# The eighth b's softmax steps placed inside the h tiles of the last stage, its F ahead of the state's first logits

## The chip, the core and the metric

The kernel runs on one core of a Trainium2 chip. The metric is the device time of one execution in microseconds; less is better. The profiled execution is read with times counted from its first instruction. Engines: PE is TensorE (matmuls), DVE is VectorE, ACT is ScalarE, POOL is GpSimd, and SP issues nearly all the transfers.

## The reference, cut to what matters

```python
# attention between x (8 b, 512 tokens, 8 heads) and a state of 32 slots per b
a  = softmax over slots (x @ state^T / 8);   xread = a @ state
a2 = softmax over tokens(state @ x^T / 8);   sread = a2 @ x
x  = concat([xread, sread])          # per b 512 tokens and 32 state rows, 8 * 544 rows of 512
# dense layer
h  = x @ w_in                        # 2048 hidden
g  = 1 if h >= 1 else 0 if h <= -1 else (h + 1)^2 / 4
x  = g @ w_out
# soft mixture: 8 experts x 4 slots = 32 slots
logits = x @ phi
d  = softmax over all rows (logits);     slot_input = d^T @ x
slot_out = relu(slot_input @ w1[e]) @ w2[e]
c  = softmax over the slots (logits);    out = c @ slot_out
```

Since x is only used through phi and through d^T, the kernel never forms g @ w_out for all rows: it forms the logits from g and w_out @ phi, and sums d^T g over the rows before w_out is applied.

## The kernel before, in words

The rows are worked on in nine stages. Stages b = 0 to 7 hold the 512 token rows of one b each; the last stage, b = 8, holds the 256 state rows of all b. Each stage has 16 **h tiles** m (128 hidden units times the stage's rows). `hstep` makes one: matmuls into one of three PSUM buffers (pool `psH`, three in turn, so h(m) takes the buffer of h(m-3)), then the activation. In the last stage an h tile is 12 matmuls of 256 columns, k = 0 to 11, since weights and x are split in a high and a low half (`wsplit` makes the halves `w` of tile m+1: a cast for the high half and a subtraction for the low half, on the engines that a table names; there are two sets, used in turn). The activation there has one of three forms; for tiles 0, 2, 3 and 4 it is a TENSOR_SCALAR on DVE (L564), a square on ACT and a SCALAR_TENSOR_TENSOR on DVE (L597); for tiles 1, 5, 6 and 7 a relu on ACT, a product on POOL (L569) and a SCALAR_TENSOR_TENSOR on DVE (L593). The DVE instruction at the end writes g and is what frees the PSUM buffer.

`estep(b, k)` (tile **E**) makes the logits of b from four g tiles; four of them sum up. `smblock(b)` then does the softmax over rows as a running one, as a generator whose steps the stage loop calls:

1. eS, a copy of the logits to SBUF on ACT;
2. **LR**: four small matmuls that turn them; DVE takes the maximum **bm** and the running maximum **nm**; ACT makes the exponentials (eS again), al = exp(old maximum - new) and the copy LT; DVE updates the running sum **sn**;
3. **dRp**: four transposes of eS on PE, and their copy **dR** on ACT;
4. `fall`, **F**: 64 matmuls of dR with the b's transposed g (tile gp), into two banks of the PSUM pool psV (FV) and two buffers of psX (FX); then eight DVE instructions fold them into **acc** (L742);
5. after the eighth b (b = 7), `merge`: D, **Mp**, nmM, al, R4a and Ra, then the matmuls **P** and **Sp** on acc and sn.

In the last stage the eighth b's steps 1 to 5 are called after h tiles 1 to 5, one each. The state's own logits E of that stage follow after tiles 5, 8, 11 and at the end; `tquarter` (tile **gtp**, eight transposes for each four g tiles, into psV) follows after tiles 5, 9, 13 and at the end.

What is written in that order is not yet each engine's order: in the last stage a list scheduler sorts the instructions of each engine by its own estimate of when they could start, so matmuls of the next h tile may stand ahead of a step. Once sorted, each engine works its list strictly in order.

The transfers all go through SP's queue, in order: F's end frees gp, into which four loads of 1 MB of expert weights go at once; P's end frees acc; the last reader of a weight tile `win`, and in the end the matmuls of the state's own sums (also named P, there reading natS) free the places of the next loads. After the last stage come the state's softmax (`smstate`), the experts on the weights as they land, and the combination, whose results are written out.

Of the kernel before, what the change touches and what calls it, by code (L numbers as in the profile page):

```python
# [13 lines left out]
PSUM = bass.MemoryType.PSUM  # L14


CFG = {'gg': 1, 'ns': 1, 'do': 0, 'no': 1, 'nl': 0, 'n0': (1, 12), 'nw': 512, 'nj': 'CABD', 'cw': (2, 2, 2, 4, 5, 6, 6, 7, 8, 8, 9, 11, 12, 13, 14, 15), 'pr': (0, 3, 4, 6), 'a0n': 4, 'w1p': (), 'r0': 3, 'sw': 1, 'whole': (6, 7), 'em': 8, 'lE': (0, 5, 8, 11), 'sV': (0, 4, 9, 12), 'sE': (7, 11, 15), 'sS': (1, 3, 5, 7), 'sN': 13, 'sM': (14, 14), 'gv7': 'EESEESSEEESSEEEE', 'cpos': (0, 0, 1, 1, 2, 2, 3, 7, 8, 9, 10, 10, 13, 14), 'at0': (4, 4, 7, 7, 9, 13, 14, 15, 15, 15), 'lP0': ((1, 1), (2, 1), (3, 1)), 'lP1': ((1, 0), (1, 1), (2, 0), (2, 1), (3, 0)), 'gv1': 'EEEEEEEEEESEEEES', 'f32': (0, 1, 2, 3), 'wsm': 14, 'xsP': 1, 'eng': ('PE',), 'wt8': (7, 8, 9, 10, 11, 12, 13, 14), 'wte': 'DA', 'wb': 12, 'gv6': (3, 5, 15), 'lP': ((0, 0), (0, 1), (1, 0), (2, 0), (3, 1)), 'attA': (3, 4, 7, 9, 9, 9, 11, 12), 'attB': (1, 11, 11, 12, 13), 'attN': (14, 15), 'dv': (3, 7, 8), 'fl': -0.484375, 'hp': 2000, 'att7': (3, 5, 6, 7, 8, 10), 'og': 1, 'n3': 1, 'n3m': 10, 'wS': ('AP', 'PP', 'AD', 'AP', 'DP', 'DP', 'PP', 'DD', 'AP', 'DP', 'AD', 'AP', 'DD', 'AD', 'DD', 'DP'), 'xsm': 12, 'k0': 0, 'rg': 6, 'spg': 0, 'att0': 6, 'att': 7, 'V0': (1, 3, 4), 'Vn': (0, 3, 9), 'Vx': 12, 'wn': 'H', 'wsev': 'adad', 'conv': (4, 8, 9, 11, 12, 13, 19, 21, 24, 26, 28, 32, 36, 40, 44, 48, 52, 56, 60), 'todo': [1, 1, 1, 2, 0, 0, 0, 3, 0, 0, 2, 2, 1, 1, 0, 0], 'E0': ((0, 8), (0, 14), (0, 14), (0, 15)), 'T0': ((0, 12), (0, 14), (0, 15), (1, 0)), 'sm0': 6, 'E': 1, 'sm': 1, 'tqB': (5, 9, 13), 'GP': 0, 'pe': (3,), 'psH': 3, 'gtpX': (0, 7), 'tq0': (13, 15), 'keep': (2, 3, 4, 5), 'x2': (1, 3), 'natm': 1, 'warm': 26, 'bounce7': (0, 3), 'split': 1, 'wt': 0, 'so': '111000000000ccc111111', 'smm': (0, 0, 1, 2, 8, 10, 12), 'tqv': (), 'tqvm': 0, 'first': 'x', 'apath': 2, 'f32c': 1, 'place': 1, 'attm': (3, 6, 7, 8, 9, 12), 'subPm': True, 'loDm': False, 'bounce': (0, 1, 2, 3), 'bq': ('s', 's'), 'xq': 's', 'nat': ((1, 11), (2, 2), (2, 3), (2, 11), (3, 2), (3, 4), (3, 9), (4, 2), (4, 3), (4, 9), (5, 2), (5, 3), (5, 9), (6, 2), (6, 4), (6, 9)), 'subP': (1,), 'mulD': (), 'loD': (), 'qlag': 0, 'gv0': 'ESSESEEESEEEEEEE', 'gv': 'EEEEEEESEEEESEEE', 'gvS': 'BEBBBEEESSSBEBBB'}


@with_exitstack  # L20
def kernel(
# [157 lines left out]
        stage_load(nxt(i))  # L179

    wps, wD = {}, {}

    def conv_wo(i):

        g, h = divmod(i - 8, 2)
        if h == 0:
            wD[g] = rot_g.tile([128, 4, 512], F32, tag="g", name="wD")
        words(i, wD[g][:, 2 * h:2 * h + 2, :].rearrange("p k f -> p (k f)"))
        stage_load(nxt(i))
        if h == 1:  # L190
# [333 lines left out]
    def hstep(b, m):  # L524
# [6 lines left out]
        elif b < B:  # L531
            vh, vl = Vt[b, c]
            ah, al = aT[b]
            f = slice(128 * mm_, 128 * mm_ + 128)
            seq = [(vh, ah), (vh, al), (vl, ah)]
            k = 0
            for G in range(2):
                for v, a in seq:
                    mm(out=h, lhsT=v[:, G, f], rhs=a[:, G, :], start=(k == 0), stop=(k == 5))  # L539
                    k += 1  # L540
        else:
            wh, wl = wS[m]
# [87 lines left out]
    def smblock(b):  # L630
# [89 lines left out]
    def fall(b, al, dR):  # L720
# [226 lines left out]
    for b in range(B + 1):  # L947
# [14 lines left out]
        for m in range(NM):  # L962
# [156 lines left out]
    def combine(dh, groups):  # L1119
# [4 lines left out]
        for n, bs in groups:  # L1124
# [80 lines left out]
```

## Time and profile before

| | us |
|---|---|
| median of 3 runs | 477.71 (477.70 to 478.51) |
| profiled execution | 476.62 |
| its span, first to last instruction | 474.8 |
| PE busy | 436.8 (92%) |
| DVE busy | 372.8 (79%) |
| ACT busy | 288.6 (61%) |
| POOL busy | 245.4 (52%) |

How to read it: "busy" is the time in which an engine has an instruction at work; PE overlaps its matmuls, so that its ends are modelled. The page cuts the span in 40 slices of 11.9 us and gives each engine's busy share in tenths. The chain of work that ended last is followed backwards from the last instruction, at each step to what released it. A row of the timeline gives start, length, engine, line and operation; what stands in brackets is the idle time before it and what ended it. Most rows name a line of a helper (L128 is every ACT instruction, L116 and L122 are matmuls issued side by side, L820 is every load of expert weights).

### The profile page before, as it was taken

The numbers are of one execution on the slowest core, as the hardware profiler recorded it, in microseconds if no ns is written. First come the engines' busy times: TensorE is split into PE (matmuls) and PEld (weight loads), VectorE is DVE, ScalarE is ACT, GpSimd is POOL, SyncE is SP. The second block draws the span as 40 slices with busy tenths as digits, with TensorE's granted clock in tenths as the row PEclk, the third lists the DMA queues.
The fourth block names the chain that finished last, engine by engine and source line by source line (L and its number), as shares of the span: only waits on it lengthen the run. The fifth ranks groups of instructions, "written<-read, shape, count | busy, mean of one in ns | idle before, by whom it ended". The sixth has DMA issues, their size and how long they took to land.

```text
span 474.8 us, 10761 instructions
## 1 busy us (share of the span) xinstructions
PE 436.8 (92%) x4352; PEld 249.5 (53%) x4352; DVE 372.8 (79%) x664; ACT 288.6 (61%) x526; POOL 245.4 (52%) x222
## 2 busy tenths in 40 slices
PE   4699999999999999999999999999999998899860
PEld 2433345455565565565556555655656786436430
DVE  2999999896999998999899999977877665350350
ACT  1868987647784875887587588545745364210350
POOL 4243347865873973796397379645247542030030
PEclk9889899999999999999999999999999999999995
DMA  8999822010403613260361326106045399999998
GB/s 300 420 420 418 362 90 90 11 80 13 167 1 135 232 79 135 90 222 10 130 247 62 134 90 233 79 19 249 1 179 186 126 373 353 342 421 418 388 357 273
DMA packets 21634, 94.21 MB, mean 198 GB/s; under 512 B 1873, under 2 KB 8401, under 8 KB 13265
## 3 DMA queue, kind: packets, MB, share of 16 engines
q1 hardware_dynamic: 21328, 93.00, 51.9%
q8 instruction: 34, 0.56, 0.5%
q0 software_dynamic: 256, 0.52, 0.4%
q14 instruction: 16, 0.12, 0.1%
HBM read 80.41 MB, written 13.11 MB: 197 GB/s over the span
## 4 chain that ended last, share of the span: by engine, by line
PE 51%; DVE 29%; DMA 7%; issue 4%; POOL 3%; ACT 2%; ACTq 0%; SPq 0%; POOLq 0%; DVEq 0%
PE h L539 19%; DMA w<-in_w_dram 6%; DVE gp L618 6%; DVE g L593 5%; PE h L547 5%; PE E L116 4%; PE FV L122 4%; PE V L116 3%; PE FX L122 2%; PE h L530 2%; POOL c L569 2%; DVE mx L295 2%; PE FV L116 1%; DVE win L173 1%; DVE z L336 1%
## 5 line engine op out<-in xcount | busy, mean ns | idle before, releaser
L539 PE MATMUL h<-a,v 128*128 128x512 f32 x672 | 175.2, 404 | 2.0 <-DVE g L593 1.7
L569 POOL TENSOR_TENSOR c<-c 128x512 f32<-128x512 f32 x107 | 116.8, 1095 | 99.7 <-ACT c L128 97.9
L539 PEld LDWEIGHTS h<-a,v 128*128 128x128 f32 x672 | 120.3, 188 | 77.2 <-issue 19.7
L128 ACT ACTIVATE c<-h,half 128x512 f32<-128x512 f32 x128 | 88.2, 690 | 71.7 <-PE h L539 55.8
L593 DVE SCALAR_TENSOR_TENSOR g<-h,c 128x512 f32<-128x512 f32 x112 | 74.7, 668 | 19.7 <-POOL c L569 16.9
L618 DVE STREAM_TRANSPOSE gp<-g 128x512 f32<-128x512 f32 x112 | 78.2, 700 | 1.2
L486 POOL TENSOR_TENSOR v<-Vs,v 128x512 fp32r<-128x512 f32 x30 | 41.7, 1389 | 9.3 <-ACT Vs L128 9.3
L128 ACT ACTIVATE v<-V 128x512 fp32r<-128x512 f32 (+1 forms) x64 | 38.1, 602 | 6.8 <-PE V L122 3.8
L116 PE MATMUL V<-win,st_t 64*32 64x512 f32 x64 | 33.4, 601 | 4.0 <-ACT att L128 3.5
L122 PE MATMUL V<-win,st_t 64*32 64x512 f32 x448 | 35.7, 601 | 0.0
L530 PE MATMUL h<-spare,v 128*128 128x512 f32 x64 | 34.0, 669 | 1.8 <-DVE gp L593 0.8
L122 PE MATMUL FX<-gp,dR 32*32 32x512 f32 x512 | 35.6, 598 | 0.0
L122 PE MATMUL FV<-gp,dR 32*32 32x512 f32 x496 | 35.4, 597 | 0.0
L122 PE MATMUL E<-g,wp 128*32 128x512 f32 x168 | 29.5, 602 | 0.0
L116 PE MATMUL E<-g,wp 128*32 128x512 f32 x56 | 29.1, 602 | 0.0
L338 POOL TENSOR_TENSOR att<-att,z 128x512 f32<-128x512 f32 x16 | 17.2, 1077 | 18.1 <-DVE z L337 18.1
L547 PE MATMUL h<-XSh,v 128*128 128x256 f32 x128 | 25.2, 289 | 0.0
L1141 DVE COPY o<-oV 128x512 f32<-128x512 f32 x6 | 4.1, 692 | 26.6 <-PE oH L122 26.5
L128 ACT ACTIVATE spare<-wb 128x512 uint8<-128x512 uint8 x32 | 23.9, 784 | 0.0
L530 PEld LDWEIGHTS h<-spare,v 128*128 128x128 f32 x64 | 12.2, 207 | 20.8 <-issue 12.9
L547 PEld LDWEIGHTS h<-XSh,v 128*128 128x128 f32 x128 | 20.3, 189 | 2.8 <-issue 1.0
L1149 POOL DMA_DIRECT2D out_dram<-o x8 | 4.1, 518 | 31.8 <-DVE o L1141 31.8
(245 smaller groups left out, 829.9 us busy)
## 6 DMA issues: line engine op xcount, KB each, us to landing
w<-in_w_dram SPq DMA_DIRECT2D x22, 1024.0 KB, 10.1
xn<-in_xn_dram SPq DMA_DIRECT2D x8, 1024.0 KB, 4.8
wb<-in_won_dram SPq DMA_DIRECT2D x8, 1024.0 KB, 5.0
xs<-in_xs_dram SPq DMA_DIRECT2D x7, 1024.0 KB, 5.1
gp<-in_w_dram SPq DMA_DIRECT2D x6, 1024.0 KB, 6.8
out_dram<-o SPq DMA_DIRECT2D x12, 512.0 KB, 6.5
gp<-in_wout_dram SPq DMA_DIRECT2D x5, 1024.0 KB, 12.2
wb<-in_win_dram SPq DMA_DIRECT2D x4, 1024.0 KB, 13.6
```

Of the source, the lines that this page charges most:

```text
L116: first = mm(**calls[0])
L122: e = mm(**c)
L128: return nc.scalar.activation(out=out, in_=in_, func=func, **kw)
L295: nc.vector.tensor_reduce(out=mx, in_=S[G], op=ALU.max, axis=AX.X)
L338: (nc.vector if b in CFG["mulD"] else nc.gpsimd).tensor_tensor(out=t3, in0=t3, in1=z1.unsqueeze(2).to_broadcast([128, 16, 32]), op=ALU.mult)
L486: nc.gpsimd.tensor_tensor(out=lo[:, G, :], in0=Vs, in1=hi[:, G, :], op=ALU.subtract)
L530: mm(out=h, lhsT=Vt[0, c][0][:, G, 128 * mm_:128 * mm_ + 128], rhs=araw[0][G], start=(G == 0), stop=(G == 1))
L539: mm(out=h, lhsT=v[:, G, f], rhs=a[:, G, :], start=(k == 0), stop=(k == 5))
L547: mm(out=h, lhsT=w[:, j, :], rhs=x[:, j, :], start=(k == 0), stop=(k == 11))
L569: nc.gpsimd.tensor_tensor(out=c, in0=c, in1=c, op=ALU.mult)
L593: gI[b, m] = nc.vector.scalar_tensor_tensor(out=g, in0=h, scalar=1.0, in1=c, op0=ALU.max, op1=ALU.min)
L618: nc.vector.transpose(out=gd_of(b, m), in_=gT[b, m])
```

## The change

Five table entries that are new (`ev`, `st`, `fa`, `fb`, `fd`) are off, and the code that they would switch on does nothing. What is left: in the last stage the eighth b's steps 2, 3 and 4 are no longer called after h tiles 2, 3 and 4 but from within an h tile's loop over its 12 matmuls, ahead of matmul k of tile m, at (2, 7), (4, 1) and (4, 10); that matmul is told to stand behind the step's last matmul on PE. Steps 1 and 5 stay after tiles 1 and 5.

```diff
-CFG = {'gg': 1, ...
+CFG = {'ev': 0, 'st': 0, 'fa': 0, 'fb': 0, 's8': ((2,7),(4,1),(4,10)), 's9': (1, 5), 'fd': (), 'gg': 1, ...
...
             for j in range(4):
                 for w, x in ((wh, xh), (wh, xl), (wl, xh)):
-                    mm(out=h, lhsT=w[:, j, :], rhs=x[:, j, :], start=(k == 0), stop=(k == 11))
+                    e = None
+                    if (m, k) in CFG["s8"]:
+                        step(run["sm"])
+                        e = run["pe"]
+                    i = mm(out=h, lhsT=w[:, j, :], rhs=x[:, j, :], start=(k == 0), stop=(k == 11))
+                    if e is not None:
+                        tc.add_manual_dep(i.ins, e.ins.name, ORDER, reason="in turn")
                     k += 1
...
-        group([dict(out=LR[32 * t:32 * t + 32, :], lhsT=R4, rhs=eS[:, 128 * t:128 * t + 128], start=True, stop=True) for t in range(T)])
+        run["pe"] = group([dict(out=LR[32 * t:32 * t + 32, :], lhsT=R4, rhs=eS[:, 128 * t:128 * t + 128], start=True, stop=True) for t in range(T)])
...
-            nc.tensor.transpose(dRp[:, r, :], eS[:, 128 * r:128 * r + 128], ident)
+            run["pe"] = nc.tensor.transpose(dRp[:, r, :], eS[:, 128 * r:128 * r + 128], ident)
...
-        group([dict(out=F[k][32 * t:32 * t + 32, :], lhsT=dR[32 * k:32 * k + 32, r, 32 * t:32 * t + 32],
+        run["pe"] = group([dict(out=F[k][32 * t:32 * t + 32, :], lhsT=dR[32 * k:32 * k + 32, r, 32 * t:32 * t + 32],
...
-                        sm = smblock(b - 1)
+                        sm = run["sm"] = smblock(b - 1)
...
-            if sm is not None and (m >= CFG["sm0"] if b == 1 else m >= CFG["sm"] if last or CFG["smm"] is None else m in CFG["smm"]):
+            if sm is not None and (m >= CFG["sm0"] if b == 1 else (m in CFG["s9"] if CFG["s8"] else m >= CFG["sm"]) if last else m in CFG["smm"]):
                 step(sm)
```

The instructions and their number stay the same on all engines; POOL's and SP's lists keep their order, and all lists are the same up to the second h tile of the last stage. In the names below h_3976, h_4003, h_4022, h_4056, h_4174, h_4243 and h_4261 are the last stage's h tiles 0, 1, 2, 3, 5, 6 and 7 in both kernels; tile 4 is h_4081 before and h_4074 now. The line numbers of the kernel now are 13 to 25 higher in these functions.

PE, last stage, where F begins. Before, tile 5 was complete, and the state's first logits (E_4190) stood ahead of F:

```order
L547 MATMUL h_4174<-XSl_3925,v0_568 128x256
L547 MATMUL h_4174<-XSh_3924,v0_568 128x256
L116 MATMUL E_4190<-s_gc_3971,wp_95 32x256
L122 MATMUL E_4190<-s_gc_3971,wp_95 32x256 x3
L116 MATMUL FV_4097<-gp_107,dR_4077 32x512
```

Now the same place of PE's list, from dRp on:

```order
L568 MATMUL h_4074<-XSh_3924,v0_568 128x256
L689 MATMUL dRp_4076<-cst_t_87,eS_101 128x128 x4
L568 MATMUL h_4074<-XSl_3925,v0_568 128x256
L568 MATMUL h_4074<-XSh_3924,v0_568 128x256 x2
L568 MATMUL h_4074<-XSl_3925,v0_568 128x256
L568 MATMUL h_4074<-XSh_3924,v0_568 128x256 x2
L568 MATMUL h_4074<-XSl_3925,v0_568 128x256
L568 MATMUL h_4074<-XSh_3924,v0_568 128x256 x2
L568 MATMUL h_4174<-XSh_3924,v0_568 128x256
L568 MATMUL h_4174<-XSl_3925,v0_568 128x256
L116 MATMUL FV_4092<-gp_107,dR_4081 32x512
```

F moved from behind tile 5 and E to behind ten matmuls of tile 4 and the first two of tile 5; the ten others of tile 5, E, and now also eight transposes gtp follow F.

DVE, last stage, the stretch from bm to the g of tile 3. Before:

```order
L520 CAST v0_568<-win1_104 128x512
L593 SCALAR_TENSOR_TENSOR s_gc_3971<-h_4003,s_gc_3971 128x256
L564 TENSOR_SCALAR s_gc_3971<-h_4022 128x256
L642 TENSOR_REDUCE bm_4043<-LR_4038 128x1
L651 SCALAR_TENSOR_TENSOR nm_4047<-bm_4043,nm_3691 128x1
L748 TENSOR_SCALAR D_4195<-cst_t_87,nm_4047 128x4
L520 CAST v0_568<-win1_104 128x512
L597 SCALAR_TENSOR_TENSOR s_gc_3971<-h_4022,s_gc_3971 128x256
L564 TENSOR_SCALAR s_gc_3971<-h_4056 128x256
L660 SCALAR_TENSOR_TENSOR sn_4051<-sn_3695,al_4046,bs_4045 128x1
```

The same stretch now (the first CAST is tile 4's high half, the second tile 5's; each is followed on POOL by the subtraction for the low half):

```order
L665 TENSOR_REDUCE bm_4035<-LR_4030 128x1
L616 SCALAR_TENSOR_TENSOR s_gc_3971<-h_4003,s_gc_3971 128x256
L674 SCALAR_TENSOR_TENSOR nm_4039<-bm_4035,nm_3691 128x1
L537 CAST v0_568<-win1_104 128x512
L587 TENSOR_SCALAR s_gc_3971<-h_4022 128x256
L771 TENSOR_SCALAR D_4195<-cst_t_87,nm_4039 128x4
L537 CAST v0_568<-win1_104 128x512
L587 TENSOR_SCALAR s_gc_3971<-h_4056 128x256
L683 SCALAR_TENSOR_TENSOR sn_4043<-sn_3695,al_4038,bs_4037 128x1
L620 SCALAR_TENSOR_TENSOR s_gc_3971<-h_4022,s_gc_3971 128x256
```

The casts stand behind bm and nm, and the instruction that ends tile 2 (reads h_4022, L597, now L620) moved from ahead of sn to behind it.

DVE, last stage, behind F's first fold into acc. Before, casts and g of tile 4 and 5 stood ahead of the fold:

```order
L597 SCALAR_TENSOR_TENSOR s_gc_3971<-h_4081,s_gc_3971 128x256
L520 CAST v0_568<-win1_104 128x512
L521 TENSOR_TENSOR v0_568<-win1_104,v0_568 128x512
L593 SCALAR_TENSOR_TENSOR s_gc_3971<-h_4174,s_gc_3971 128x256
L742 SCALAR_TENSOR_TENSOR acc_97<-acc_97,al_4046,FV_4097 128x8x32 x4
```

Now:

```order
L765 SCALAR_TENSOR_TENSOR acc_97<-acc_97,al_4038,FX_4094 128x8x32 x2
L587 TENSOR_SCALAR s_gc_3971<-h_4074 128x256
L537 CAST v0_568<-win1_104 128x512
L538 TENSOR_TENSOR v0_568<-win1_104,v0_568 128x512
L620 SCALAR_TENSOR_TENSOR s_gc_3971<-h_4074,s_gc_3971 128x256
```

Tile 4's activation and both halves of tile 7's weights moved behind the fold.

## Rows read from the trace of the kernel before

**Rows 1.** The page, 40 slices: busy tenths of PE and of the DMA engines.
```profile
PE   4699999999999999999999999999999998899860
DMA  8999822010403613260361326106045399999998
```

**Rows 2.** Stretches: busy us (count) of PE, PEld, DVE, ACT, POOL; clock; DMA share; GB/s.
```profile
406.50:407.50 1.00, 0.73 (x7) 0.36 (x4) 0.48 (x1) 0.33 (x1) 0.00 (x0) 1.00 0.37 156
409.50:441.00 31.50, 30.10 (x382) 14.26 (x374) 8.96 (x14) 5.08 (x11) 5.14 (x3) 1.00 1.01 409
```

**Rows 3.** SP's queue: its longest wait from 395 to 415 us, and two issues.
```profile
SPq L820 <- PE P L122: 6.0, 1, 6.0
...
379.47 0.33 SPq L820 DMA_DIRECT2D gp<-in_w_dram  x1
...
406.73 0.33 SPq L820 DMA_DIRECT2D w<-in_w_dram  x1
```

**Rows 4.** The chain that ended last, 367 to 390 us: start, us, what.
```profile
367.46 1.85 PE h L547 x14
369.31 0.23 PE LR L116
...
369.67 2.80 PE h L547 x22
372.47 0.44 PE dRp L666 x4
372.90 1.52 PE h L547 x12
374.43 0.33 PE E L116
...
375.00 0.54 PE FV L116
...
379.39 3.03 PE h L547 x24
382.42 0.65 PE gtp L613 x6
...
386.93 1.18 PE h L547 x10
...
389.38 0.71 PE h L547 x6
```

**Rows 5.** Timeline of POOL, the low halves of tiles 4 and 5 (L521), and an earlier product.
```profile
133.41 1.05 POOL L338 TENSOR_TENSOR att<-att,z 128x512 f32<-128x512 f32 x1
...
369.57 1.28 POOL L521 TENSOR_TENSOR v<-win,v 128x512 fp32r<-128x512 f32 x1 [0.62 <-DVE v L520]
371.63 1.29 POOL L521 TENSOR_TENSOR v<-win,v 128x512 fp32r<-128x512 f32 x1 [0.79 <-DVE v L520]
```

**Rows 6.** Timeline of DVE, instructions beside those of POOL, and the fold.
```profile
133.45 1.02 DVE L651 SCALAR_TENSOR_TENSOR nm<-bm,nm 128x1 f32<-128x1 f32 x1
...
369.00 0.43 DVE L520 CAST v<-win 128x512 fp32r<-128x512 f32 x1 [1.34 <-PE h L547]
...
369.67 0.42 DVE L564 TENSOR_SCALAR s_gc<-h 128x256 f32<-128x256 f32 x1
370.00 0.28 DVE L642 TENSOR_REDUCE bm<-LR 128x1 f32<-128x128 f32 x1
...
372.04 0.90 DVE L660 SCALAR_TENSOR_TENSOR sn<-sn,al,bs 128x1 f32<-128x1 f32 x1
...
379.40 1.66 DVE L742 SCALAR_TENSOR_TENSOR acc<-acc,al,FV 128x256 f32<-128x256 f32 x4 [2.89 <-PE FX L122]
...
382.54 0.72 DVE L520 CAST v<-win 128x512 fp32r<-128x512 f32 x1
...
385.56 0.68 DVE L521 TENSOR_TENSOR v<-win,v 128x512 fp32r<-128x512 f32 x1
```

**Rows 7.** Lines of DVE over the run: shortest, median and longest ns.
```profile
L660 DVE SCALAR_TENSOR_TENSOR sn<-sn,al,bs x7: 170/173/897, 136.3 to 372.0; 128x1 f32<-128x1 f32 x7
```

More of the change, by code (lines that the diff above doesn't have):

```diff
@@ new lines @@
+CFG = {'ev': 0, 'st': 0, 'fa': 0, 'fb': 0, 's8': ((2,7),(4,1),(4,10)), 's9': (1, 5), 'fd': (), 'gg': 1, 'ns': 1, 'do': 0, 'no': 1, 'nl': 0, 'n0': (1, 12), 'nw': 512, 'nj': 'CABD', 'cw': (2, 2, 2, 4, 5, 6, 6, 7, 8, 8, 9, 11, 12, 13, 14, 15), 'pr': (0, 3, 4, 6), 'a0n': 4, 'w1p': (), 'r0': 3, 'sw': 1, 'whole': (6, 7), 'em': 8, 'lE': (0, 5, 8, 11), 'sV': (0, 4, 9, 12), 'sE': (7, 11, 15), 'sS': (1, 3, 5, 7), 'sN': 13, 'sM': (14, 14), 'gv7': 'EESEESSEEESSEEEE', 'cpos': (0, 0, 1, 1, 2, 2, 3, 7, 8, 9, 10, 10, 13, 14), 'at0': (4, 4, 7, 7, 9, 13, 14, 15, 15, 15), 'lP0': ((1, 1), (2, 1), (3, 1)), 'lP1': ((1, 0), (1, 1), (2, 0), (2, 1), (3, 0)), 'gv1': 'EEEEEEEEEESEEEES', 'f32': (0, 1, 2, 3), 'wsm': 14, 'xsP': 1, 'eng': ('PE',), 'wt8': (7, 8, 9, 10, 11, 12, 13, 14), 'wte': 'DA', 'wb': 12, 'gv6': (3, 5, 15), 'lP': ((0, 0), (0, 1), (1, 0), (2, 0), (3, 1)), 'attA': (3, 4, 7, 9, 9, 9, 11, 12), 'attB': (1, 11, 11, 12, 13), 'attN': (14, 15), 'dv': (3, 7, 8), 'fl': -0.484375, 'hp': 2000, 'att7': (3, 5, 6, 7, 8, 10), 'og': 1, 'n3': 1, 'n3m': 10, 'wS': ('AP', 'PP', 'AD', 'AP', 'DP', 'DP', 'PP', 'DD', 'AP', 'DP', 'AD', 'AP', 'DD', 'AD', 'DD', 'DP'), 'xsm': 12, 'k0': 0, 'rg': 6, 'spg': 0, 'att0': 6, 'att': 7, 'V0': (1, 3, 4), 'Vn': (0, 3, 9), 'Vx': 12, 'wn': 'H', 'wsev': 'adad', 'conv': (4, 8, 9, 11, 12, 13, 19, 21, 24, 26, 28, 32, 36, 40, 44, 48, 52, 56, 60), 'todo': [1, 1, 1, 2, 0, 0, 0, 3, 0, 0, 2, 2, 1, 1, 0, 0], 'E0': ((0, 8), (0, 14), (0, 14), (0, 15)), 'T0': ((0, 12), (0, 14), (0, 15), (1, 0)), 'sm0': 6, 'E': 1, 'sm': 1, 'tqB': (5, 9, 13), 'GP': 0, 'pe': (3,), 'psH': 3, 'gtpX': (0, 7), 'tq0': (13, 15), 'keep': (2, 3, 4, 5), 'x2': (1, 3), 'natm': 1, 'warm': 26, 'bounce7': (0, 3), 'split': 1, 'wt': 0, 'so': '111000000000ccc111111', 'smm': (0, 0, 1, 2, 8, 10, 12), 'tqv': (), 'tqvm': 0, 'first': 'x', 'apath': 2, 'f32c': 1, 'place': 1, 'attm': (3, 6, 7, 8, 9, 12), 'subPm': True, 'loDm': False, 'bounce': (0, 1, 2, 3), 'bq': ('s', 's'), 'xq': 's', 'nat': ((1, 11), (2, 2), (2, 3), (2, 11), (3, 2), (3, 4), (3, 9), (4, 2), (4, 3), (4, 9), (5, 2), (5, 3), (5, 9), (6, 2), (6, 4), (6, 9)), 'subP': (1,), 'mulD': (), 'loD': (), 'qlag': 0, 'gv0': 'ESSESEEESEEEEEEE', 'gv': 'EEEEEEESEEEESEEE', 'gvS': 'BEBBBEEESSSBEBBB'}
@@ L181 @@
     wps, wD = {}, {}
+    pend = []
     def conv_wo(i):
@@ L196, in conv_wo, with over @@
             wpp = wps[g][:, 0:128].rearrange("p (x n) -> p x n", x=4)
-            for x in range(4):
-                mm(out=wpp[:, x, :], lhsT=sb[:, 128 * x:128 * x + 128], rhs=R4, start=True, stop=True)
-            act(wp[:, 4 * g:4 * g + 4, :], wpp)
+            def over():
+                for x in range(4):
+                    mm(out=wpp[:, x, :], lhsT=sb[:, 128 * x:128 * x + 128], rhs=R4, start=True, stop=True)
+                act(wp[:, 4 * g:4 * g + 4, :], wpp)
+            if g in CFG["fd"]:
+                pend.append(over)
+            else:
+                over()
     def nat_load(u, at):
@@ L263, with warm @@
     araw = {}
-    def warm(n):
+    def warm(n, after=None):
         w = psE.tile([128, 128], F32, tag="E", name="warm")
-        for _ in range(n):
-            mm(out=w, lhsT=xs_s[:, 1920:2048], rhs=xs_s[:, 1920:2048], start=True, stop=True)
+        with tc.high_priority(CFG["hp"] if after is not None else 0):
+            for _ in range(n):
+                x = ident if after is not None else xs_s[:, 1920:2048]
+                i = mm(out=w, lhsT=x, rhs=x, start=True, stop=True)
+                if after is not None:
+                    tc.add_manual_dep(i.ins, after.ins.name, ORDER, reason="in turn")
+                    after = i
     def attention(b):
@@ L324, in turn @@
                 for st in range(4):
-                    nc.tensor.transpose(p[:, st, :], e2[G][:, 128 * st:128 * st + 128], ident)
+                    i = nc.tensor.transpose(p[:, st, :], e2[G][:, 128 * st:128 * st + 128], ident)
+                if b == 0 and G == 0 and CFG["fa"]:
+                    warm(CFG["fa"], i)
                 t = e2[G].rearrange("p (a x) -> p a x", a=4)
@@ L468, in vchunk @@
         P2 = [slice(64 * G, 64 * G + 64) for G in range(2)]
-        group([dict(out=V[G][32 * j:32 * j + 32, :], lhsT=st_t[P2[G], b, j, :], rhs=win_t[c][P2[G], j, :],
-                    start=True, stop=True) for j in range(4) for G in range(2)])
+        i = group([dict(out=V[G][32 * j:32 * j + 32, :], lhsT=st_t[P2[G], b, j, :], rhs=win_t[c][P2[G], j, :],
+                        start=True, stop=True) for j in range(4) for G in range(2)])
+        if (b, c) == (0, 1) and CFG["fb"]:
+            warm(CFG["fb"], i)
         if b == 0 and c in CFG["f32"]:
@@ L973 @@
             hstep(b, m)
+            while pend:
+                pend.pop()()
             nat(b, m)
@@ L1137, in combine @@
                 v = ps[t][:, 0:W * nb].rearrange("p (b d) -> p b d", b=nb)
-                if n_ev % 2:
+                if t > 1 if CFG["ev"] and T == 4 else n_ev % 2:
                     act(o[:, t], v)
@@ L1145, in combine @@
                     dma(out=out[544 * b:544 * b + 512, dc].rearrange("(p t) d -> p t d", t=4), in_=o[:, :, i])
+                elif CFG["st"]:
+                    ob = out.rearrange("(t q n) d -> n q t d", t=2, q=4)
+                    for q in range(4):
+                        dma(out=ob[512:544, q, :, dc], in_=o[32 * q:32 * q + 32, :, 0])
                 else:
```

1 line of the change is left out of this document (removed).

## The prediction

> **What bounds the kernel now.** I read the page's slices first: PE is at nine tenths from the third slice to about 390 us and hardly less to 400, the DMA engines from about 380 us to the end [rows 1]. So there is one bound in the middle, PE, and another at the end, the transfers of the expert weights and results, and the question is how the second hangs on the first. The stretches say it: between 406.5 and 407.5 us the DMA share falls to 0.37, and from 409.5 to 441 it is 1.01 [rows 2]. The engines ran dry once and were full afterwards. The reader is to see in SP's waits why: its next load stood 6.0 us waiting for the matmuls P, and went out at 406.73 [rows 3]. Every load behind it, and all results, follow that moment with full engines. The end is therefore the time of the state's P plus a fixed sum of bytes, and what comes before 406.7 in the transfers can be earlier without use.
>
> What sets P? The chain of waits from 367 to 390 us is PE alone, piece after piece, with no other engine between [rows 4]; and PE stays at nine tenths up to 400 us [rows 1]. So a microsecond that PE loses or saves in the last stage moves the end by the same microsecond.
>
> **PE's own work.** The same matmuls are done in another order. An h matmul costs 1.18 / 10 = 0.118 us, and coming back to h costs about 0.2 us behind F and LR (3.03 - 24 x 0.118 and 2.80 - 22 x 0.118) and 0.1 behind dRp (1.52 - 12 x 0.118) [rows 4]. LR, dRp and F each still interrupt the h tiles once. E no longer leads straight to F, but to gtp, behind which there was no such cost either. I put this at 0, with 0.2 us to either side. So nothing is gained on PE itself, and the change pays only if waits go. There are none on PE's chain here to go.
>
> **What the early F gives.** PE's lists are the same up to tile 2, at 367.46. LR stands five matmuls earlier: 369.31 - 0.59 = 368.72, ends 0.36 later, at 369.08. Then 16 matmuls (2.09) to dRp at 371.17, dRp 0.43, and nine matmuls (1.16) until tile 5 is to begin, at 372.76; two of its matmuls later F could start, at 373.0 instead of 375.00 [rows 4]. If nothing waits, F's end and the four loads of gp, issued at 379.47 before [rows 3], come about 1.9 us earlier. By the first part this is worth 0 at the end: it widens the dry spell at 406.5.
>
> **First new wait: tile 5 for tile 2's buffer.** There are three PSUM buffers, so tile 5 needs the DVE instruction that ends tile 2. Before, this stood ahead of sn in DVE's list; now it stands behind it. What sn can cost is in the trace: it took 0.90 us at 372.04, and ended at 372.94, within 0.02 us of the end of POOL's subtraction (371.63 + 1.29) [rows 5, 6]; the middle one of its seven took 0.17 [rows 7]. The running maximum nm at 133.45 did the same: 1.02 us, ending 0.01 us behind a POOL product [rows 5, 6]. These small instructions wait out whatever POOL is doing.
>
> Now the times. bm can start at 369.15, and bm (0.28), the g of tile 1 (0.42, as its like at 369.67) and nm (0.17 as an undisturbed sn, POOL being idle there) put tile 4's cast at 370.02 instead of 369.00 [rows 6, 7]. It ends at 370.45; POOL's subtraction starts 0.14 behind a cast (369.57 against 369.43) and runs 370.59 to 371.87 [rows 5, 6]. Tile 5's cast comes next on DVE, meets that subtraction, and ends at about 372.2: the cast at 382.54, which met one too, took 0.72 instead of 0.43, so 0.29 from POOL's end to its own is my estimate. POOL's second subtraction then runs 372.3 to 373.6, and sn, which has one 0.42 us instruction between it and that cast, reaches DVE's head at 372.6, inside it. So sn ends at 373.6, tile 2's buffer is free at 374.0, and tile 5, wanted at 372.76, waits **1.2 us**. Behind that matmul on PE's list stand F and everything else. F starts at 374.2 and ends at 378.6: 0.8 us earlier than before, not 1.9.
>
> If sn met no POOL instruction it would take 0.17, and the wait would be 0.45; if tile 5's cast lost another 0.4 us to POOL, 1.6. I take 1.2, since the row with the same neighbours (cast, subtraction on POOL, sn) is the one at 372.04.
>
> No row shows whether D, which now stands ahead of tile 5's cast, waits for POOL as well. The Trainium skill says in SBUF - State Buffer, section Who interferes with whom, that a tensor_scalar from SBUF to SBUF can take the port pair that VectorE shares with GpSimd and that whoever comes second blocks fully, as does an instruction with two SBUF inputs against a reading GpSimd. By that D too would hold the cast back to POOL's end, the cast would end at 372.3 instead of 372.2, and the wait would be 1.3; for sn and nm the trace agrees.
>
> **Second new wait: tile 7 for tile 4's buffer.** Behind F, DVE folds for 3.14 us (379.40 to 382.54), as before. But tile 4's TENSOR_SCALAR (0.42), tile 7's cast (0.43) and subtraction (0.68) and the g of tile 4 (0.42) now follow the fold [rows 6]: 5.1 us from F's end to tile 4's buffer. PE needs from F's end to tile 7: twelve h matmuls (1.61), E (0.57), eight gtp (0.87, from 0.65 for six), tile 6 (1.42) and Mp (0.1, estimated from one gtp transpose): 4.6 to 4.7 us, with 0.2 more if the returns cost something [rows 4]. Tile 7 waits **0.4 us**. It is 0 with the returns and faster DVE starts, and 0.9 if the cast and the subtraction meet POOL (0.3 each). gtp needs the FV banks, free 1.66 us behind F; PE gets there after 2.2, so this one is covered.
>
> **The sum.** 1.2 + 0.4 + 0 = 1.6 us. Against its own time the profiled execution goes from 476.62 to 478.2; the median of the runs lies 1.09 above that execution, so the median goes from 477.71 to 479.3. The ends are 0.45 + 0 = 0.5 and 1.6 + 0.9 = 2.5: 478.2 to 480.2.
>
> **The rivals.** (1) Faster: the transfers, not P, set the end, and the gp loads' lead counts. With the wait of tile 5 this lead is 0.8 us, 476.9; without it 1.9, 475.8. For it: DMA at nine tenths from 380 us on. Against it: the dry spell of rows 2 and the 6.0 us wait of rows 3, which a lead only makes longer. The Trainium skill says in SBUF - State Buffer, section A bandwidth-pool intuition that's wrong, that HBM is almost always the end-to-end bottleneck; by this rule the lead would count in full. The trace agrees only from 409 us on. Chance 0.07.
>
> (2) No change that can be measured: the waits are there but small, because sn reaches DVE ahead of POOL's second subtraction, or PE reaches tile 5 later than I think. Then 0 to 0.45 for the first wait and 0 to 0.4 for the second: 477.7 to 478.6, likeliest 478.3. It is decided by whether sn starts inside the subtraction; there are 0.3 us between them. Chance 0.27.
>
> (3) Slower still: behind the merge POOL has two subtractions (tiles 8 and 9) and two products (tiles 6 and 7) in a row, all fed later now. If they come late, tile 9 or the second E waits for up to one subtraction more, 1.3 us: 480.6. For it: the nm and al that feed them are behind tile 4's g now. Against it: P and Sp give PE's list over a microsecond there. Chance 0.12.
>
> **How the numbers follow.** The forecast has 0.54, with 478.2 to 480.2 as its own range. The range for 8 in 10 runs from 477.6, into rival 2, to 480.5, nearly to rival 3; below it lie rival 1 and little of rival 2, above it half of rival 3. A measurement of this kernel tells about 0.2% from no change, that is 476.75 to 478.67. Faster: rival 1, 0.07. Same: rival 2 and the low end of the forecast, less rival 2's upper end, 0.28. Slower: 0.65.
>
> **What the profile of the changed kernel would show.** Right: sn long (1 us) and ending with a POOL subtraction; a gap on PE of 1.2 us ahead of tile 5, put down to DVE, and one of 0.4 ahead of tile 7; F from about 374.2; the first gp load at 378.7; the ten h matmuls that began at 386.93 begin at 388.5; SP's load behind P at 408.3 instead of 406.73, with a longer dry spell ahead of it. Wrong: no gap ahead of tile 5 and sn at 0.2 us (rival 2), or DMA never dry between 398 and 409 us and the end earlier (rival 1). A P that comes later while the end does not move would break the first part, on which all else stands.

## The result, and the profile after

| | before | after |
|---|---|---|
| median | 477.56 | 482.12 |
| profiled execution | 476.62 | 480.13 |
| its span | 474.8 | 478.3 |
| PE busy | 436.8 | 435.8 |
| DVE busy | 372.8 | 372.4 |
| POOL busy | 245.4 | 245.7 |

The medians are those of the runs made beside each other (the two kernels in turn, on one chip). The changed kernel is slower: the ratio of the times is 1.0094, with an interval of 1.0075 to 1.0114, that is 4.5 us (3.6 to 5.4). The prediction had said 479.3, and 480.5 as its upper end: the sign was right, the size too small. The busy times are the same to 1 us, so nothing is computed at more cost; what is lost is order. The page's slices of after (span, busy tenths of PE and of the transfers, 11.96 us each) against [rows 1]:

```profile
span 478.3 us, 10758 instructions
PE   4679999999999999999999999999999997999870
DMA  8999822010403613351361346025056397999898
```

The reader is to see two places.

**The last stage.** DVE's and POOL's timelines of after (start, us, engine, line, operation, tiles; in brackets the idle time before and what ended it), against [rows 5, 6]:

```profile
369.25 0.29 DVE L665 TENSOR_REDUCE bm<-LR 128x1 f32<-128x128 f32 x1 [1.48 <-PE LR L122]
...
369.88 0.43 DVE L537 CAST v<-win 128x512 fp32r<-128x512 f32 x1
...
370.56 1.20 DVE L771 TENSOR_SCALAR D<-cst_t,nm 128x4 f32<-128x4 f32 x1
371.68 0.41 DVE L537 CAST v<-win 128x512 fp32r<-128x512 f32 x1
...
372.35 1.21 DVE L683 SCALAR_TENSOR_TENSOR sn<-sn,al,bs 128x1 f32<-128x1 f32 x1
373.48 0.74 DVE L620 SCALAR_TENSOR_TENSOR s_gc<-h,s_gc 128x256 f32<-128x256 f32 x2
378.85 1.66 DVE L765 SCALAR_TENSOR_TENSOR acc<-acc,al,FV 128x256 f32<-128x256 f32 x4 [4.63 <-PE FX L122]
380.42 1.65 DVE L765 SCALAR_TENSOR_TENSOR acc<-acc,al,FX 128x256 f32<-128x256 f32 x4
381.99 0.42 DVE L587 TENSOR_SCALAR s_gc<-h 128x256 f32<-128x256 f32 x1
382.32 0.42 DVE L537 CAST v<-win 128x512 fp32r<-128x512 f32 x1
382.85 0.69 DVE L538 TENSOR_TENSOR v<-win,v 128x512 fp32r<-128x512 f32 x1
383.45 0.42 DVE L620 SCALAR_TENSOR_TENSOR s_gc<-h,s_gc 128x256 f32<-128x256 f32 x1
```

```profile
370.45 1.29 POOL L538 TENSOR_TENSOR v<-win,v 128x512 fp32r<-128x512 f32 x1 [1.39 <-DVE v L537]
372.26 1.28 POOL L538 TENSOR_TENSOR v<-win,v 128x512 fp32r<-128x512 f32 x1 [0.52 <-DVE v L537]
```

sn takes 1.21 us, and ends at 373.56, 0.02 behind POOL's second subtraction (372.26 + 1.28 = 373.54). D, of which no row of before told, does the same with the first one: 1.20 us, to 371.76 against 371.74. Behind sn come the g of tiles 2 and 3, in one row; the first of them frees tile 2's buffer, and only then PE goes on. Two rows of PE's timeline of after, tile 5 and tile 7:

```profile
373.95 0.39 PE L568 MATMUL h<-XSh,v 128*128 128x256 f32 x1 [0.95 <-DVE s_gc L620]
...
383.93 0.39 PE L568 MATMUL h<-XSh,v 128*128 128x256 f32 x1 [0.22 <-DVE s_gc L620]
```

The h matmuls before them started at 372.72 and 383.42, and one follows another by 0.12, so tile 5 waited 373.95 - 372.84 = 1.11 us and tile 7 383.93 - 383.54 = 0.39. From the first h matmul behind E<-g to tile 10 PE took 21.74 us before (367.39 to 389.13) and takes 23.72 now (367.50 to 391.22). The P of the state then starts 1.95 us later, counted from SP's last load before this stretch (406.83 - 367.83 against 404.77 - 367.72), and SP's load behind it stands at 408.79 in place of 406.73 [rows 3].

**The end of the program.** From there the transfers were full before until the results were out. Now they run dry once more. Stretches of 2 us (busy us and count of PE, PEld, DVE, ACT, POOL; clock; DMA share; GB/s), of before and then of after:

```profile
446.00:448.00 2.00, 2.00 (x26) 1.01 (x19) 1.29 (x2) 1.19 (x2) 0.00 (x0) 1.00 0.93 352
448.00:450.00 2.00, 1.98 (x27) 0.81 (x25) 0.00 (x0) 0.60 (x1) 0.00 (x0) 1.00 1.04 356
450.00:452.00 2.00, 1.04 (x6) 0.61 (x10) 0.00 (x0) 0.77 (x2) 0.00 (x0) 1.00 1.04 351
```

```profile
448.00:450.00 2.00, 2.00 (x29) 1.07 (x27) 2.00 (x4) 1.52 (x3) 0.00 (x0) 1.00 0.43 180
450.00:452.00 2.00, 2.00 (x29) 1.09 (x24) 1.47 (x3) 1.16 (x3) 0.00 (x0) 1.00 0.59 196
```

Between 448 and 452 the share misses 0.57 x 2 + 0.41 x 2 = 2.0 us of transfer, where before it missed 0.1. The loads have all been issued, and no result is there to be written: SP issues the first one at 449.59, against 445.34 before, 4.25 us later although the loads are only 2.06 later. SP's timeline, of before and then of after:

```profile
445.34 23.09 SPq L1145 DMA_DIRECT2D out_dram<-o  x14
```

```profile
449.59 23.10 SPq L1170 DMA_DIRECT2D out_dram<-o  x14
```

The reason stands in PE's list, in a part that the diff does not touch. In the last experts, SO are the matmuls on a tile of weights (one tile w for each expert), SR sums the first half of them up, and oV, oX, oH and oE combine it into results. PE's list there, before and after ("..." stands for the rest of the first two groups, the same in both):

```
L1097 MATMUL SO<-w_8_4618,hTD 32x256 x2
L1106 MATMUL SR<-tail,cst_t 128x256
L1097 MATMUL SO<-w_9_4626,hTD 32x256 x8
L116 MATMUL oV<-tail,LT 128x256
...
L1097 MATMUL SO<-w_10_4632,hTD 32x256 x5
```

```
L1122 MATMUL SO<-w_8_4618,hTD 32x256 x2
L1122 MATMUL SO<-w_9_4626,hTD 32x256 x8
L1131 MATMUL SR<-tail,cst_t 128x256
L1122 MATMUL SO<-w_10_4632,hTD 32x256 x4
L116 MATMUL oV<-tail,LT 128x256
...
L1122 MATMUL SO<-w_10_4632,hTD 32x256 x4
```

SR now stands behind the matmuls on w_9, and the first two groups behind the first matmuls on w_10. Both of these wait for their load, with work behind them that could have been done. PE's timeline shows it, of before and then of after:

```profile
439.90 0.70 PE L1106 MATMUL SR<-tail,cst_t 128*128 128x256 f32 x2
441.33 1.07 PE L1097 MATMUL SO<-w,hTD 128*32 128x256 f32 x16 [0.73 <-DMA w<-in_w_dram]
442.33 0.48 PE L116 MATMUL oV<-tail,LT 32*128 32x256 f32 x1
```

```profile
443.47 1.07 PE L1122 MATMUL SO<-w,hTD 128*32 128x256 f32 x16 [1.44 <-DMA w<-in_w_dram]
444.47 0.70 PE L1131 MATMUL SR<-tail,cst_t 128*128 128x256 f32 x2
446.00 0.64 PE L1122 MATMUL SO<-w,hTD 128*32 128x256 f32 x8 [0.83 <-DMA w<-in_w_dram]
446.57 0.48 PE L116 MATMUL oV<-tail,LT 32*128 32x256 f32 x1
```

So there are two candidates: PE's 2.0 us in the last stage, and the re-sorted end, some 2 us. The experiments separate them and take the first one apart.

### The profile page after: what moved, and what is told of

Same layout as the page of the kernel before. It is cut to its first block, busy times and chain, and to the rows that moved or that the text cites. A ratio compares the mean times of both kernels' runs of the same rounds, so it can differ in the third digit from the quotient of the medians.

```text
span 478.3 us, 10758 instructions
## 1 busy us (share of the span) xinstructions
PE 435.8 (91%) x4352; PEld 248.1 (52%) x4352; DVE 372.4 (78%) x664; ACT 288.3 (60%) x526; POOL 245.7 (51%) x222
## 4 chain that ended last, share of the span: by engine, by line
PE 47%; DVE 31%; DMA 9%; issue 4%; POOL 3%; ACT 3%; SPq 0%; ACTq 0%; POOLq 0%; DVEq 0%
PE h L556 19%; DVE gp L641 6%; DMA wb<-in_win_dram 6%; DVE g L616 5%; PE h L568 4%; PE E L116 4%; PE FV L122 4%; DMA w<-in_w_dram 4%; PE h L1087 3%; PE V L116 3%; PE FX L122 2%; DVE wD L173 2%; POOL c L592 2%; DVE att L311 2%; PE FV L116 1%
## 5 line engine op out<-in xcount | busy, mean ns | idle before, releaser
L116 PE MATMUL V<-win,st_t 64*32 64x512 f32 x64 | 34.2, 615 | 4.4 <-ACT att L128 3.7
L122 PE MATMUL V<-win,st_t 64*32 64x512 f32 x448 | 36.6, 615 | 0.0
L547 PE MATMUL h<-spare,v 128*128 128x512 f32 x64 | 30.9, 614 | 3.4 <-DVE gp L616 3.2
L547 PEld LDWEIGHTS h<-spare,v 128*128 128x128 f32 x64 | 11.2, 192 | 20.9 <-issue 10.5
```

The costliest lines, as they stand in the source:

```text
L116: first = mm(**calls[0])
L122: e = mm(**c)
L547: mm(out=h, lhsT=Vt[0, c][0][:, G, 128 * mm_:128 * mm_ + 128], rhs=araw[0][G], start=(G == 0), stop=(G == 1))
```

## The experiments

**Theory A**: both losses are real and add; each microsecond by which the state's P comes later is one at the end, and the new order at the end costs another 2 us. **Theory B** (the rival): the end is late only because the loads are, and its order hardly matters; or the order matters only with late loads.

**1. a_tail, the changed kernel with two places of the end as before.** SR is pinned ahead of the matmuls on w_9, the first two groups ahead of those on w_10.

```diff
-                if dh and "c0" in run and ft == 0 and CFG["do"]:
-                    tc.add_manual_dep(i.ins, run["c0"].ins.name, ORDER, reason="in turn")
+                if dh and ft == 0 and e in (1, 2):
+                    tc.add_manual_dep(i.ins, run["SR0" if e == 1 else "c2"].ins.name, ORDER, reason="in turn")
```

> The changed kernel with the last stage as changed, but PE's order behind it put back as before: the row sum SR ahead of the weights w_9, and the first two groups of the combination ahead of w_10. Theory 1 (two separate losses: about 2.0 us of waits on PE in the last stage, and about 2.4 us because PE's list puts the first results behind one more load): 479.6, and the transfers no longer run dry at 449 to 451 us. Rival (the dry spell only follows from the late last stage, its order costs nothing by itself): 482.

Measured: 480.66, against 477.23 before, ratio 1.0067 (1.0042 to 1.0091). This is between the two expectations. The dry stretch at 448 is gone, but there is another at 456 to 460, in a_tail's stretches:

```profile
456.00:458.00 2.00, 1.44 (x12) 0.39 (x10) 1.56 (x3) 0.84 (x2) 0.00 (x0) 1.00 0.81 275
458.00:460.00 2.00, 1.92 (x20) 1.05 (x18) 1.34 (x3) 0.73 (x2) 1.37 (x3) 1.00 0.52 211
```

It misses 0.38 + 0.96 = 1.3 us. Two pins are not the old order: the groups of the second half still stood elsewhere. With 2.0 for the late P this makes 3.3 of the 3.43 measured, but it was not yet a clean test.

**2. b_late, the kernel before with those two places of the end as in the changed kernel.** The mirror of a_tail: nothing else is touched.

```diff
+                if dh and e == 1 and ft == 7:
+                    tc.add_manual_dep(run["SR0"].ins, i.ins.name, ORDER, reason="in turn")
+                if dh and e == 2 and ft == 3:
+                    for x in run["cf"]:
+                        tc.add_manual_dep(x.ins, i.ins.name, ORDER, reason="in turn")
```

> The kernel before with its last stage untouched, and only PE's order behind it taken from the changed kernel: SR behind w_9, the first two groups of the combination behind half of w_10. Theory 1: about 2.4 us slower than before, 480.0, with a dry spell of the transfers of 2 us before the first result. Rival: as before, 477.6, since the last stage is not late.

Measured: 478.68 against 477.23, ratio 1.003 (1.0013 to 1.0047): 1.45 us of loss with the state's P where it was (37.01 us behind SP's last load before it; 37.05 in the kernel before). So the order alone costs time, less than the 2.4 that I had put on it.

**3 and 4. a_sn and a_sn_d: a_tail, and sn, or sn and D, behind a g on DVE.** In a_sn the eighth b's sum stands behind the g of tile 2, for which tile 5 waits; in a_sn_d sn and D both stand behind the g of tile 3.

```diff
+        if b == B - 1:
+            e = nc.vector.scalar_tensor_tensor(out=run["s"], in0=so, scalar=al, in1=bs, op0=ALU.mult, op1=ALU.add)
+            tc.add_manual_dep(e.ins, gI[B, 2].ins.name, ORDER, reason="in turn")
```

> As a_tail, and sn of the eighth b stands behind the instruction that ends tile 2 on DVE, instead of ahead of it. Theory 1 (sn, which waits out POOL's subtraction, holds tile 2's buffer): the gap ahead of tile 5 goes, F starts 1.1 us earlier, and the time is 1.1 less than that of a_tail, 478.5. Rival (the casts and D behind nm are what makes tile 5 wait; sn is only the last in a row): less than 0.3 us gained, 479.4.

> As a_sn, and D too is held back, sn and D both behind the instruction that ends tile 3. Theory 1: with sn gone from the way, D costs PE nothing; time as a_sn, 478.5, and tile 5's cast starts as late as before, since it now meets POOL's subtraction itself. Rival (D holds the cast and with it PE): another 0.5 to 1 us gained, 477.8.

Measured: 479.56, ratio 1.0052 (1.0032 to 1.0072), and 479.52, ratio 1.0048 (1.0025 to 1.0072). Both are 1.1 us below a_tail, and above what was expected by the 1 us that a_tail itself was; P stands 0.80 and 0.76 us later than before, where in a_tail it was 1.97. So sn's place is worth 1.1 to 1.2 us, and moving D away too gains nothing more.

**5 and 6. a_full and b_atail: the whole order at the end, exchanged.** All 188 TensorE instructions of SO, SR and the groups are chained in the order that the other kernel has; a_full is the changed kernel with the end of the kernel before, b_atail the kernel before with the end of the changed one.

```diff
+    for x, y in zip(TAIL, TAIL[1:]):
+        tc.add_manual_dep(tl[y].ins, tl[x].ins.name, ORDER, reason="in turn")
```

(`tl` holds the 188 instructions as written, `TAIL` their places in the other kernel's list.)

> The changed kernel with all 188 TensorE instructions of the two matmul-and-combine ends (SO, SR, oV, oX, oE, oH) chained in the order that they have in the kernel before; the first remedy, a_tail, had fixed only two places of that list and its transfers still ran dry at 457 to 459. Theory A (the loss is two things: 2.0 us of TensorE's waits in the last stage, passed on one to one, and the re-sorted end, 1.4 to 3 us): before + 2.0, 479.2, and no dry stretch of the transfers between 446 and 470. Theory B (the end is late for another reason, such as the later loads themselves, and its order was a minor part): as a_tail, before + 3.2 to 3.4, 480.5, with a dry stretch again.

> The kernel before with one thing changed: the 188 TensorE instructions of the matmul-and-combine ends stand in the order that they have in the changed kernel. Nothing of the last stage is touched. Theory A (the two losses add: 4.5 us in all, 2.0 of them TensorE's waits): before + 2.0 to 2.6, with a dry stretch of the transfers around 446 to 450. Theory B (the new order only hurts where the last loads come 2 us late, so most of it needs the waits): before + 0.7 or less. In b_late the part of that order that stood out first cost 1.45.

Measured: a_full 478.89 against 476.93, ratio 1.0043 (1.0027 to 1.006), that is 1.96 us; b_atail 478.89 against 476.82, ratio 1.0046 (1.0025 to 1.0066), 2.07 us. Theory A twice, and theory B falls: the order costs its 2 us also with the loads on time. The sum, 4.03, is inside the interval of the changed kernel (3.6 to 5.4). A kernel whose list is chained in its own order was not run; a_full, which is chained too, loses no more than its P is late (1.96 us). The stretches of a_full show no dry one, those of b_atail do (a_full first):

```profile
448.00:450.00 2.00, 2.00 (x23) 1.07 (x18) 1.29 (x2) 1.20 (x2) 0.00 (x0) 1.00 0.94 345
450.00:452.00 2.00, 1.71 (x26) 0.67 (x24) 0.00 (x0) 0.82 (x2) 0.00 (x0) 1.00 1.05 359
```

```profile
446.00:448.00 2.00, 2.00 (x36) 1.26 (x28) 1.48 (x3) 0.76 (x2) 0.00 (x0) 1.00 0.83 344
448.00:450.00 2.00, 2.00 (x31) 1.25 (x30) 1.47 (x3) 1.40 (x3) 0.00 (x0) 1.00 0.27 101
```

b_atail misses 0.34 + 1.46 = 1.8 us there. From here on every kernel has the old end, so that only the last stage differs.

**7. a_sn_full: a_full, and sn behind the g of tile 2.**

> a_full, and the update of the eighth b's sum sn put behind g of tile 2 on VectorE, so that tile 5 no longer waits for it. In a_sn tile 10 began 22.6 us behind the group's first anchor, against 22.0 in the kernel before and 23.9 in the changed kernel. Theory A: what is left of TensorE's loss is 0.6 us, so before + 0.6, 477.8. Theory B (a_sn's other loss stays): before + 2.0 or more, 479.3.

Measured: 477.82 against 476.93, ratio 1.0017 (0.9997 to 1.0037), 0.9 us; P is 0.82 later. Tile 5's wait was worth 1.1 us, as PE's timeline had it.

**8. a_Fold: a_full, with F back in its old place behind tile 4.** LR and dRp stay inside tiles 2 and 4.

```diff
-'s8': ((2,7),(4,1),(4,10)), 's9': (1, 5)
+'s8': ((2,7),(4,1)), 's9': (1, 4, 5)
```

> a_full, but F back in its old place behind tile 4; LR and dR stay inside tiles 2 and 4. The build then puts c and g of tile 4 ahead of F's accumulations on VectorE again, as in the kernel before. Theory A: the wait of tile 5 stays (1.2 to 1.5 us), that of tile 7 goes (0.5 to 0.8): before + 1.3, 478.5. Rival (F's place has no part in it, all comes from sn and D behind the subtraction on GpSimd): as a_full, 479.2.

Measured: 478.11 against 476.93, ratio 1.0031 (1.0012 to 1.0049), 1.2 us; P is 1.21 later. The build puts the c and g of tile 4 ahead of F's fold on DVE again, and tile 7's wait is gone. So by P F's new place costs 0.75 us (the two times alone, 0.78 apart, would not show it, since their intervals overlap), and of what it was to bring, the earlier loads of gp, no gain is seen.

**9. a_fix: a_sn_full, and DVE's fold of F split around tile 4's c and g**, so that tile 7 does not wait either. F keeps its new place.

```diff
+                    if b == B - 1:
+                        accs.append(e)
...
+                tc.add_manual_dep(e.ins, accs[1].ins.name, ORDER, reason="in turn")
+                tc.add_manual_dep(accs[2].ins, e.ins.name, ORDER, reason="in turn")
...
+            tc.add_manual_dep(gI[b, m].ins, accs[3].ins.name, ORDER, reason="in turn")
+            tc.add_manual_dep(accs[4].ins, gI[b, m].ins.name, ORDER, reason="in turn")
```

> a_sn_full, and on VectorE the eight accumulations of F are split around tile 4's two steps (c of tile 4 behind the second, g of tile 4 behind the fourth), so that tile 7 no longer waits either. F still stands in its new place. Theory A (an early F is worth nothing by itself): before + 0 to 0.3, 477.2 to 477.5. Rival L (the lead of some 2 us that the gp loads then have is worth something at the end): 0.5 us or more below the kernel before, 476.7 or less. Rival C (an early F collides with something else): before + 1 or more.

Measured: 477.48 against 476.93, ratio 1.0018 (1.0003 to 1.0034), 0.55 us. The first load of gp went out at 377.52, 1.8 us earlier than before counted from SP's load at 367, and the time did not fall below that of the kernel before. Rival L is not borne out; but P came 1.07 later, and with an interval from 0.14 us up, a lead worth as much as 0.9 us is not excluded by this run. P is late although no h tile waits for a g in this trace: other waits took the place of those that were removed. Timelines of a_fix:

```profile
379.38 0.86 DVE L780 SCALAR_TENSOR_TENSOR acc<-acc,al,FV 128x256 f32<-128x256 f32 x2
380.30 1.09 PE L647 MATMUL gtp<-cst_t,s_gc 128*128 128x128 f32 x8
386.21 1.28 POOL L543 TENSOR_TENSOR v<-win,v 128x512 fp32r<-128x512 f32 x1
387.15 0.27 PE L647 MATMUL gtp<-cst_t,s_gc 128*128 128x128 f32 x1
387.54 0.50 PE L573 MATMUL h<-XSh,v 128*128 128x256 f32 x2
```

With the fold split, its last part on FV ends at 380.24, and gtp, which goes into the same pool psV, starts 0.06 behind it and 0.29 behind the h matmul ahead of it, where 0.12 is usual: a wait of 0.17. Tile 9's first matmul on the low half of its weights starts at 387.54, 0.05 behind the end of POOL's subtraction (387.49) and 0.39 behind gtp, where 0.03 is usual: a wait of 0.36. Tile 4 waits 0.15 in the same way; this wait, which the changed kernel has too, is taken up below. Together they are 0.7 of the 1.07. So a_fix is no kernel without waits, and it does not test an early F by itself.

**10. a_dd: a_full, and POOL's second subtraction given to DVE.** The cause of sn's 1.21 us by itself.

```diff
-'wS': ('AP', 'PP', 'AD', 'AP', 'DP', 'DP', ...
+'wS': ('AP', 'PP', 'AD', 'AP', 'DP', 'DD', ...
```

> a_full, and one of the two subtractions that ran on GpSimd beside the eighth b's steps, the one at 372.26 of the changed kernel's trace, done by VectorE (0.7 us). Theory A (sn, a sum of 128 x 1, took 1.21 us only because it waited for GpSimd's subtraction to end): sn now takes 0.15 to 0.25, and D, whose subtraction stays on GpSimd, still 1.20; VectorE comes to g of tile 2 some 0.3 us earlier, so the time is a_full's less 0.3: before + 1.7. Rival (sn waits for something else, its own operands from ScalarE among them): sn still ends 1 us or more after it was begun, and the time is a_full's plus 0.4 to 0.7.

Measured: 477.69 against 476.82, ratio 1.0019 (1.0 to 1.0037), 0.9 us. DVE's timeline of a_dd:

```profile
370.16 1.21 DVE L776 TENSOR_SCALAR D<-cst_t,nm 128x4 f32<-128x4 f32 x1
...
371.95 0.20 DVE L688 SCALAR_TENSOR_TENSOR sn<-sn,al,bs 128x1 f32<-128x1 f32 x1
372.08 0.68 DVE L543 TENSOR_TENSOR v<-win,v 128x512 fp32r<-128x512 f32 x1
372.69 0.74 DVE L625 SCALAR_TENSOR_TENSOR s_gc<-h,s_gc 128x256 f32<-128x256 f32 x2
```

With nothing on POOL beside it sn takes 0.20; D, whose subtraction is still there, 1.21. That is the cause shown by itself. The time fell by more than the 0.3 expected, since the build also put F ahead of tile 5's first two matmuls, so that F no longer stood behind the waiting one; how much of the gain is owed to that was not tried apart. Tile 7 still waits some 0.15 us in a_dd: the pair of h matmuls at 381.82 that takes in its first one lasts 0.65, where such a pair behind a wait lasts 0.50.

## Why the prediction was wrong

By its own steps:

**What bounds the kernel.** Half right. That a microsecond of P is one at the end was borne out as far as the runs can tell: P later by 1.96, 1.21, 0.82, 1.07 and 0.51 us gave 1.96, 1.18, 0.89, 0.55 and 0.87 (a_full, a_Fold, a_sn_full, a_fix, a_dd), all inside their intervals, which are 1.5 to 1.9 us wide. But **the step "Every load behind it, and all results, follow that moment with full engines" failed**. It is true of the kernel before, whose transfers only just stay full (0.93 between 446 and 448), because its first results are made while the last loads are on their way. The prediction took this as a property of the stage's bytes. It hangs on PE's list at the end, and that list had changed: the scheduler sorts by its own estimate of when things could start, and an edit in the last stage moves these estimates for all that follows (this cause of the new order is argued, its price is shown). The prediction spoke of the order only where the diff stood. This is 2.1 us (b_atail) of a miss of 2.9 (4.5 measured, 1.6 forecast). The profiled executions show it too: from SP's load behind P to the end of the span it was 68.1 us before and 67.2 to 68.0 in the five kernels that have the whole old end (a_full, a_sn_full, a_Fold, a_fix, a_dd), but 69.5 in the changed kernel and 69.5 in b_atail, whose P is on time.

**First wait, tile 5.** Right in size and cause: 1.11 us measured against 1.2. The sum was worked out row by row: sn inside POOL's second subtraction, end of sn 373.56 (373.6 forecast), F from 374.38 (374.2). D, left open, did wait out POOL's first subtraction, 1.20 us, as the Trainium skill's SBUF - State Buffer, section Who interferes with whom, has it for a tensor_scalar from SBUF to SBUF; a_dd's D and sn agree with it row by row. What that did to the sum was small, since the cast behind D would have waited for POOL as well.

**Second wait, tile 7.** Right too: 0.39 measured, 0.4 forecast.

**PE's own work, put at 0.** Wrong by 0.5 us, and this is the second step that failed. Of the 1.98 us that PE lost up to tile 10, the two waits are 1.50. LR, dRp, F, E, P and Sp take what they took, by the starts in the timelines (E 1.14, F 4.39, P 1.0), and gtp 0.07 more; the 96 h matmuls take 14.39 us in place of 12.48, 0.4 more than the waits. Part of this is a third wait, which the sum left out:

```profile
371.45 0.36 PE L568 MATMUL h<-XSl,v 128*128 128x256 f32 x1
371.80 0.50 PE L568 MATMUL h<-XSh,v 128*128 128x256 f32 x2
```

The second row begins with tile 4's first matmul on the low half of its weights. It starts 0.06 behind the end of POOL's subtraction that makes this half (370.45 + 1.29 = 371.74), and 0.35 behind the matmul ahead of it, where 0.20 is usual behind a return to h: a wait of 0.15. The prediction had this subtraction in time, to 371.87, but let it hold only tile 5's cast and ran tile 4 through. In the changed kernel the wait is hidden: tile 5's, behind it, ends when DVE is done, and is only shorter by as much. It counts where tile 5 does not wait, as in a_fix and a_dd. Each of the three waits also costs some 0.1 behind its end, where the next matmul follows by 0.22 in place of 0.12 (374.17 - 373.95); and PE comes back to h seven times now, five before, since Mp and single gtp transposes now break tiles apart, at some 0.08 each time by the starts in the timelines. These terms come to 0.6; where the changed kernel gains the rest of it back was not followed. All this is worked out from rows, and no run put any of these terms alone to the test. a_dd fits: with tile 4's wait and 0.15 at tile 7, its P is 0.51 later.

**What the early F gives, 0.** Borne out as far as the runs tell: in a_sn_full and a_fix, with gp's loads 1.8 us earlier, the time was not below the kernel before. It is not a sharp test, since P was later in both (0.82 and 1.07) and the intervals begin at -0.1 and 0.1 us. F's new place alone (a_full against a_Fold) is a loss of 0.75 us of P and 0.8 of time.

**The rivals.** The first, faster by the lead, fell with this. The Trainium skill's rule that it drew on (SBUF - State Buffer, A bandwidth-pool intuition that's wrong) fits this case only from 409 us on, where the transfers are full (share 1.01 in [rows 2]; these rows do not tell whether HBM or the DMA engines fill up). Of an earlier load ahead of that point no gain was seen. The second fell by the two waits. The third named POOL's later work, and 480.6; no wait of tile 9 or of the second E stands in the trace of the changed kernel (one of 0.36 at tile 9 does in a_fix). None of the rivals was the one that happened.

So the sum should have read 1.1 + 0.4 + 0.5 + 2.1 = 4.1 where it read 1.2 + 0.4 + 0 + 0 = 1.6. What is left to the 4.5 measured is inside the interval (3.6 to 5.4).

## What to carry to other kernels

Where a scheduler sorts the lists, an edit changes every list behind it: compare the whole order of each engine to its end, and read most closely the places where the transfers are just full. An instruction that waits for a load should have nothing behind it that is ready; in an in-order list two groups of matmuls on the wrong side of a load were worth 1.45 us (b_late), the whole order of the end 2.07 (b_atail). And a one-column update on VectorE is not small beside a GpSimd operation: put it behind what TensorE waits for, and look also at what a matmul in the middle of a tile needs, not only at its first.

## What the runs showed of the hardware that was not expected

- D, a tensor_scalar of 128 x 4 elements, took 1.20 us (1.21 in a_dd and 1.22 in a_fix) beside a subtraction on POOL, and the cast of 128 x 512 at 385.53 in after took 1.23 us beside another (385.20 + 1.28), where the like at 382.32 took 0.42. sn took 0.20 when POOL was idle.
- TensorE's granted clock fell in three of the profiled executions (a_sn, a_Fold and a_dd) in the state's softmax: in a_dd it was 0.50 between 406 and 408 us, the lower level of 1.2 GHz, and SP's load stood 3.54 us behind the start of P (408.53 - 404.99), against 1.96 in before. In a_fix it stayed at 1.00. The stretches of a_dd and then of a_fix:

```profile
404.00:406.00 2.00, 1.31 (x14) 0.78 (x18) 0.86 (x4) 0.73 (x4) 0.00 (x0) 0.79 1.04 416
406.00:408.00 2.00, 2.00 (x24) 0.85 (x16) 0.48 (x1) 0.00 (x0) 0.00 (x0) 0.50 0.51 213
```

```profile
404.00:406.00 2.00, 0.60 (x10) 0.41 (x14) 1.25 (x6) 1.30 (x5) 0.00 (x0) 1.00 1.04 434
406.00:408.00 2.00, 2.00 (x34) 0.92 (x26) 0.75 (x2) 0.00 (x0) 0.00 (x0) 1.00 0.70 295
```

PE was busy for 1.31 us of the 2 us in which the clock fell, and for 0.60 where it did not fall, so these rows do not tell what decides it. The 1.6 us did not come out whole at the end of the same executions either: from that load to the end of the span it was 67.3 us in a_dd and 67.2 in a_Fold, against 68.0 in a_fix. Why, stays open, and so does whether the clock fell in the executions of these kernels that were not profiled.
